# A feed-forward product in seven half-size products in place of eight

## The chip, the cores and the metric

The kernel runs on one core of a Trainium2 chip. A core has TensorE for matmuls, VectorE, ScalarE and GpSimd for elementwise work, SyncE for issuing transfers, a working memory of 128 partitions (SBUF), and eight accumulator banks (PSUM) of 128 partitions by 512 f32, into which TensorE writes. The metric is device time in microseconds; lower is better.

## The reference

A cross attention between tokens and states is followed by a two-layer feed-forward block. Cut to what matters, with B = 8 batches, H = 8 heads, S = 512 tokens, N = 32 states a head, D = 64:

```python
# x (8, 8, 512, 64), state (8, 8, 32, 64)
a = softmax(x @ state.T / 8)              # over the 32 states
xread = a @ state                         # (8, 8, 512, 64)
a2 = softmax(state @ x.T / 8)             # over the 512 tokens
sread = a2 @ x                            # (8, 8, 32, 64)
rows = concat([xread, sread], axis=2)     # 544 rows a batch, 4352 in all
X = rows.transpose(0, 2, 1, 3).reshape(4352, 512)
h = X @ w_in                              # w_in (512, 2048)
g = maximum(h, 0) + alpha * minimum(h, 0)
out = g @ w_out                           # w_out (2048, 512), out f32
```

## The kernel before

**Tiling.** The token rows of a batch are never formed as xread. Per batch the kernel computes `m` = states times `w_in` (a 256 x 2048 matrix, heads in two groups of 128 rows), and the first product is `m` transposed times the attention weights. The hidden layer lies transposed: for each of 16 blocks `jc` of 128 hidden units, a PSUM bank `h` of 128 units x 512 tokens. ScalarE writes `neg` = relu(-h), VectorE adds `neg` times (1 - alpha) to `h` and rounds to f16 (`gt`). The second product takes 128 tokens (a quarter `q`) at a time: 16 matmuls over `jc` sum into one bank of 128 x 512, which is copied to `osb` and stored. The state reads of all batches are collected in `XS` (256 rows) and pass through the same two layers as a ninth batch (`B`, number 8).

**Steps.** The order of all work is written out by hand in `ORDER`, a list of tokens such as `S.1.2.0.0` (step, batch, quarter, part, bank). Tokens are emitted one after the other; each engine runs its own instructions in that order and waits on semaphores for data and for free buffers. The PSUM bank of a tile is the last number of a token. The steps that the change and the prediction touch:

- `lx0`, `lx`, `lst`, `wi`, `wo`: loads of x, states and weights, all issued from GpSimd's queue (L161 to L203).
- `Z`: matmuls on zeros in the head, in units of 128 columns (L217).
- `xt`, `xo`: x of the first two batches transposed on TensorE (L287) and copied (L292, L295); `xd`: later batches, by a DMA transpose on SP.
- `sc` (L307), then for the tokens' softmax `sb` transpose, `smax`, `ssh`, `sexp`, `ssum`, `snorm`, `wb` (L340 to L376): VectorE, with `ssh` and `snorm` on GpSimd (L354, L368) and `sexp` on ScalarE.
- for the states' softmax `tm` (L388), `te` (L399), `tsum` (L409), `tn` (L413, a product of the weights with 1/sum on GpSimd), `tt` (DMA transpose on SP), `rd` (L432, state reads), `rdo` (L443).
- `m` (L457) and its casts `mo` (L479, on ScalarE `a` or VectorE `v`).
- `F`, `f`: first product (L490, L511; L499 for the reads); `N`: `neg` (L522); `G`: the PReLU (L530).
- `S`: two of the 16 matmuls of a quarter (L542); `O`: its copy and store (L580); `R`, `RO`: the same for the reads (L590, L600); `L`, `LO`: batch 7's last quarter in pieces of 256, 128 and 128 columns (L562, L573).

**Buffers.** Tiles take their PSUM bank by name (`k0` to `k5`, and one pair). `osb`, `neg` and `xg` have four buffers each, `m` seven.

Of the kernel before, what the change touches and what calls it, by code (L numbers as in the profile page):

```python
# [12 lines left out]
ALU = mybir.AluOpType  # L13
# [4 lines left out]
stc lx0.0 lx0.1 oma id Z.1.24 stt.0 Z.2.13 xt.0.0.0.1 sto.a xt.0.1.0.2 xo.0.0.0.v lst xo.0.1.0.v  # L18
Z.0.6 sc.0.0 xt.0.1.1.3 xt.0.0.1.4 sb.0.0 xo.0.0.1.v smax.0.0 xo.0.1.1.a str.0.5 sc.0.1 str.1.0 wi.0
sro.0.a lx.1 wi.1 ssh.p.0.0 sb.0.1 Z.1.3 sc.0 Z.5.7 m.0.0.1.2 sro.1.a sexp.0.0 smax.0.1 m.3.0.3.4  # L20
ssh.p.0.1 tm.0 mo.0.0.a.1 sexp.0.1 ssum.0.0 m.1.0.5.0 ssum.0.1 te.0.1 te.0.0 mo.1.0.v.1 wo.0
mo.1.0.a.0 snorm.p.0.0 mo.3.0.a.1 Z.2.23 xt.1.1.1.2 xt.1.0.1.2 xt.1.1.0.0 xt.1.0.0.0 mo.0.0.a.0
snorm.p.0.1 wb.0.0 mo.3.0.a.0 m.2.0 f.0.0.0.5 f.0.1.0.4 wi.2 mo.2.0.a.0 wb.0.1 mo.2.0.a.1 f.0.1.1
xo2.1.0.v N.0.1 m.0.1.1.3 f.0.0.1 mo.0.1.a.1 m.1.1 N.0.0 xo2.1.1.v mo.0.1.v.0 f.0.2.0.0 F.0.3.2
f.0.2.1 F.0.4.1 mo.1.1.v.0 mo.1.1.a.1 F.0.7.3 G.0.1 N.0.2 G.0.0 wo.1 F.0.5.4 N.0.3 G.0.2 wi.3 m.4.0
N.0.4 S.0.0.0.5 N.0.5 G.0.3 tsum.0 S.0.1.0.0 N.0.7 mo.4.0.a.1 G.0.4 S.0.0.1 S.0.1.1 G.0.5 mo.4.0.a.0
tn.0.1 m.0.2.2.1 sc.1 G.0.7 S.0.2.0.4 mo.0.2.a.0 tm.1 m.1.2.2.3 wo.2 tn.0.0 mo.0.2.a.1 mo.1.2.a.0
S.0.2.1 F.0.6.1 F.0.9.2 sb.1 lx.2 S.0.0.2 wo.3 S.0.1.2 S.0.2.2 xd.2 mo.1.2.a.1 F.0.8.3 N.0.6 N.0.9
te.1.1 G.0.6 smax.1 F.0.11.1 S.0.0.3 te.1.0 G.0.9 N.0.8 m.0.3 N.0.11 F.0.10.2 mo.0.3.a.0 S.0.1.3
# [24 lines left out]
rd.3.1 rd.2.3 O.2.0.a mo.6.0.v.1 mo.5.1.a.0 m.4.1.4.0 mo.5.1.a.1 mo.6.0.v.0 sc.5 rdo.3.a m.4.3.2.1
mo.4.1.a.1 S.2.3.6 F.3.11.0 rdo.2.a mo.4.3.a.0 wb.4 N.3.11 mo.4.1.a.0 S.2.2.0.3 F.3.0.2 mo.4.3.v.1
F.3.10.1 S.2.3.7 tm.5 S.2.2.1 S.2.2.2 G.3.11 N.3.0 F.4.1.4 sb.5 F.3.5.0 S.2.2.3 N.3.10 N.4.1 O.2.3.a
N.3.5 S.2.2.4 G.3.10 G.3.0 F.3.7.1 F.4.11.5 F.4.7.2 lx.6 G.4.1 N.4.11 N.3.7 S.2.2.5 S.2.2.6 smax.5
te.5.0 N.4.7 S.3.3.0.4 lx.7 S.2.2.7 G.3.5 ssh.p.5 S.3.3.1 O.2.2.a te.5.1 S.3.3.2 G.4.7 F.4.5.0
F.3.15.3 N.4.5 G.3.7 N.3.15 G.4.11 tn.4.0 F.4.4.2 G.4.5 S.3.1.0.1 F.3.12.5 S.3.3.3 N.4.4 G.3.15
G.4.4 N.3.12 G.3.12 sexp.5 F.4.6.0 N.4.6 S.3.3.4 ssum.5 F.4.8.3 S.3.1.1 F.4.3.2 S.3.1.2 F.4.0.5  # L60
S.3.3.5 S.3.3.6 N.4.3 S.3.3.7 N.4.8 G.4.6 N.4.0 S.3.1.3 S.3.1.4 xd.6 S.3.1.5 G.4.8 F.4.9.0 G.4.3
F.4.2.3 G.4.0 S.3.0.0.2 N.4.9 S.3.0.1 S.3.0.2 N.4.2 tsum.5 O.3.3.v S.3.1.6 G.4.9 S.3.0.3 sc.6 G.4.2
m.5.3.5.4 m.5.0.0.3 tm.6 snorm.p.5 S.3.0.4 S.3.0.5 mo.5.0.a.0 S.3.1.7 mo.5.0.a.1 mo.5.3.v.0 sb.6
mo.5.3.a.1 F.4.10.0 S.3.2.0.3 N.4.10 F.4.14.5 S.3.2.1 S.3.2.2 S.3.2.3 wb.5 N.4.14 S.3.0.6 tt.4
S.3.0.7 tn.5.1 F.5.3.4 O.3.1.a G.4.14 te.6.1 te.6.0 S.3.2.4 G.4.10 O.3.0.a m.7.2.1.5 m.5.2.0.2
# [39 lines left out]
def kernel(  # L105
# [38 lines left out]
    def single(k, name, shape, dtype):  # L144
        return ps.tile(shape, dtype, name=name, tag=f"k{k}", bufs=1)

    def two(name, shape, dtype):
        return ps.tile(shape, dtype, name=name, tag="two", bufs=1)
# [503 lines left out]
```

## Time and profile before

| | us |
|---|---|
| three runs, median (lowest to highest) | 217.57 (217.44 to 217.98) |
| span of the profiled execution | 216.3 |
| TensorE busy | 208.6 |
| VectorE busy | 164.8 |
| ScalarE busy | 137.6 |
| GpSimd busy | 71.1 |

The profile shows one execution. Of the profiled execution the span, from its first to its last instruction, is given; the time of the runs lies 1.3 us above it. "Busy" is the union of an engine's instruction intervals. A matmul's own length (379 ns for 512 columns) is longer than the spacing of matmuls in a row, as they are pipelined, so rates are read from runs of matmuls in the chain of work that ended last. PE is TensorE, PEld its weight loads, DVE is VectorE, ACT is ScalarE, POOL is GpSimd, SP is SyncE. A group line gives the busy time and mean ns of one instruction, and behind the second bar the idle time before them and what ended it.

### The profile page before, as it was taken

How to read it: one execution, taken by the hardware profiler on the slowest of the kernel's cores; microseconds unless marked ns; L12 is line 12 of the kernel's file. 1: busy time of each engine (PE TensorE's matmuls, PEld its weight loads, DVE VectorE, ACT ScalarE, POOL GpSimd, SP SyncE). 2: the span in 40 equal slices, each digit the busy share in tenths (PEclk: the TensorE clock that was granted, in tenths of full speed). 3: DMA queues.
4: the chain of work that ended last, by engine and by line, in shares of the span. 5: the costliest groups of instructions: out<-in, count | busy, mean ns of one | idle time of the engine just before them, and what ended most of it. 6: DMA issues, size and time to landing. Idle time of an engine off the chain costs nothing.

```text
span 216.3 us, 4190 instructions
## 1 busy us (share of the span) xinstructions
PE 208.6 (96%) x1637; PEld 99.3 (46%) x1637; DVE 164.8 (76%) x253; ACT 137.6 (64%) x271; POOL 71.1 (33%) x58
## 2 busy tenths in 40 slices
PE   7689999999999999999999999999999999999994
PEld 2433334444544444544444445444454455554553
DVE  3699988799999998999886869876798466665001
ACT  3399995998768957879449865566545346544021
POOL 7373858232367626314620112903500000000000
PEclk9999999999999999999999999999999999999999
DMA  6999999888475849596032532031430011110124
GB/s 82 165 202 203 205 187 184 107 240 141 47 129 167 109 88 194 100 192 149 18 83 97 134 63 100 2 97 50 52 147 27 25 48 48 48 48 4 48 100 145
DMA packets 39716, 23.12 MB, mean 107 GB/s; under 512 B 22144, under 2 KB 35984, under 8 KB 39696
## 3 DMA queue, kind: packets, MB, share of 16 engines
q0 software_dynamic: 12704, 8.62, 28.6%
q1 hardware_dynamic: 26960, 14.23, 25.4%
q8 instruction: 13, 0.21, 0.4%
q14 instruction: 7, 0.06, 0.1%
q10 hardware_dynamic: 32, 0.01, 0.0%
HBM read 17.31 MB, written 8.91 MB: 121 GB/s over the span
## 4 chain that ended last, share of the span: by engine, by line
PE 90%; DMA 5%; POOL 2%; issue 1%; ACT 0%; POOLq 0%
PE o L542 50%; PE h L490 25%; DMA w_in_sb<-in_moe_w_in_dram 5%; PE m_ps L457 4%; PE h L499 3%; PE o L590 3%; PE sr_ps L432 2%; PE o L562 2%; PE sc L307 1%; POOL xg L178 1%; POOL xg L161 0%; PE h L511 0%; POOL w_in_sb L197 0%; POOL st L191 0%; POOL ident masks.py:199 0%
## 5 line engine op out<-in xcount | busy, mean ns | idle before, releaser
L542 PE MATMUL o<-w_out_sb,gt 128*128 128x512 f16 x496 | 125.4, 379 | 0.0
L522 ACT ACTIVATE neg<-h 128x512 f32<-128x512 f32 (+1 forms) x144 | 77.6, 582 | 44.5 <-PE h L490 36.3
L530 DVE SCALAR_TENSOR_TENSOR gt<-neg,oma_sb,h 128x512 f16<-128x512 f32 x128 | 89.4, 737 | 18.7 <-ACT neg L522 18.3
L542 PEld LDWEIGHTS <-gt 128*128 128x128 f16 x496 | 47.5, 98 | 54.9 <-issue 2.9
L490 PE MATMUL h<-aT,m 128*128 128x512 f16 x250 | 68.7, 379 | 0.0
L490 PEld LDWEIGHTS <-m 128*128 128x128 f16 x250 | 24.1, 98 | 28.7 <-issue 0.9
L479 ACT CAST m<-m_ps 128x512 f16<-128x512 f32 x49 | 27.0, 603 | 6.4 <-PE m_ps L457 6.0
L413 POOL TENSOR_SCALAR e<-e,r 128x512 f16<-128x512 f16 x16 | 24.9, 1565 | 15.0 <-DVE r L409 13.8
L354 POOL TENSOR_TENSOR ts<-ts,mx 128x1024 f32<-128x1024 f32 (+1 forms) x9 | 15.5, 1719 | 42.2 <-DVE mx L348 42.2
L368 POOL TENSOR_TENSOR an<-ts,r 128x1024 f16<-128x1024 f32 (+1 forms) x9 | 15.4, 1720 | 25.2 <-DVE r L365 16.6
L580 ACT COPY osb<-o 128x512 f32<-128x512 f32 x23 | 13.7, 595 | 14.7 <-PE o L542 14.6
L457 PE MATMUL m_ps<-w_in_sb,stT 64*32 64x512 f16 x256 | 11.3, 383 | 0.5 <-DMA w_in_sb<-in_moe_w_in_dram 0.5
L399 ACT ACTIVATE e<-sc,nb 128x512 f16<-128x512 f32 x16 | 11.1, 704 | 0.4 <-DVE nb L391 0.4
L479 DVE CAST m<-m_ps 128x512 f16<-128x512 f32 x15 | 9.9, 677 | 1.4 <-PE m_ps L457 1.3
L530 DVE SCALAR_TENSOR_TENSOR gs<-neg,oma_sb,h 128x256 f16<-128x256 f32 x16 | 7.5, 476 | 4.5 <-ACT neg L522 4.5
L388 DVE TENSOR_REDUCE nb<-sc 128x2 f32<-128x1024 f32 x8 | 9.7, 1212 | 1.2 <-PE sc L307 1.2
L376 DVE STREAM_TRANSPOSE aT<-an 128x1024 f16<-128x1024 f16 (+1 forms) x9 | 10.0, 1115 | 0.7 <-POOL an L368 0.7
L364 DVE TENSOR_REDUCE r<-ts 128x32 f32<-128x1024 f32 (+1 forms) x9 | 9.8, 1089 | 0.7 <-ACT ts L360 0.7
L348 DVE TENSOR_REDUCE mx<-ts 128x32 f32<-128x1024 f32 (+1 forms) x9 | 9.8, 1090 | 0.0
L499 PE MATMUL h<-XS,w_in_sb 128*128 128x256 f16 x64 | 9.4, 273 | 0.0
L600 DVE COPY osr<-o 128x512 f32<-128x512 f32 x1 | 0.7, 692 | 11.3 <-PE o L590 11.3
L360 ACT ACTIVATE ts<-ts 128x1024 f32<-128x1024 f32 (+1 forms) x9 | 8.7, 971 | 0.0
(52 smaller groups left out, 117.6 us busy)
## 6 DMA issues: line engine op xcount, KB each, us to landing
out_dram<-osb SPq DMA_DIRECT2D x27, 256.0 KB, 2.4
xg<-in_x_dram POOLq DMA_DIRECT2D x7, 512.0 KB, 7.2
w_in_sb<-in_moe_w_in_dram POOLq DMA_DIRECT2D x4, 512.0 KB, 9.0
w_out_sb<-in_moe_w_out_dram POOLq DMA_DIRECT2D x4, 512.0 KB, 8.0
out_dram<-osb SPq DMA_DIRECT2D x9, 128.0 KB, 2.0
xg<-in_x_dram POOLq DMA_DIRECT2D x2, 256.0 KB, 4.9
out_dram<-osr SPq DMA_DIRECT2D x2, 256.0 KB, 2.5
st<-in_state_dram POOLq DMA_DIRECT2D x1, 224.0 KB, 5.6
```

What stands on the lines that cost most here:

```text
L354: engine(e).tensor_tensor(ts, ts, over_blocks(cols(live["mx", b], j, S // N)), ALU.subtract)
L368: engine(e).tensor_tensor(blocks(cols(live["an", b], j, S)), blocks(cols(live["ts", b], j, S)), over_blocks(cols(live["r1", b], j, S // N) ...
L399: nc.scalar.activation(live["e2", b][:, g, :, :], live["sc", b][:, :, :, g, :].rearrange("p r j s -> p (r j) s"), EXP, bias=live["nb", b][ ...
L413: nc.gpsimd.tensor_scalar_mul(e2, e2, live["r2", b][:, g : g + 1])
L457: nc.tensor.matmul(t[N * k : N * (k + 1), :], st_head(b, h)[64 * r : 64 * r + 64, :], w_in_sb[64 * r : 64 * r + 64, c, 512 * f : 512 * (f ...
L479: copier(e)(m_tile(b)[:, f, g, :], live["mp", b, f][g])
L490: nc.tensor.matmul(h.rearrange("p (r j s) -> p r j s", r=2, j=2), ms[b][:, f, g, 128 * j : 128 * (j + 1)], weights(b, g), start=(g == 0), ...
L499: nc.tensor.matmul(h, w_in_sb[:, c, 128 * jc : 128 * (jc + 1)], XS[:, c].rearrange("p q n b -> p (q n b)"), start=(c == 0), stop=(c == n_c ...
L522: nc.scalar.activation(neg, h, RELU, bias=0.0, scale=-1.0)
L530: nc.vector.scalar_tensor_tensor(gt, negs.pop((b, jc)), oma_sb[:, jc : jc + 1], h, ALU.mult, ALU.add)
L542: nc.tensor.matmul(outs[b, q], gts[b, jc][:, 128 * q : 128 * (q + 1)], w_out_sb[:, jc, :], start=(jc == 0), stop=(jc == n_jc - 1),)
L580: copier(e)(osb, t)
```

## The change

1. **Second product.** For batches 1 to 7 and the reads, two quarters (`qa`, `qb`), two halves of the hidden units (low, high) and two halves of the output columns are taken as a 2 x 2 by 2 x 2 block product, in seven products of 128 tokens x 1024 hidden units x 256 columns in place of eight. With A11 = (qa, low), A12 = (qa, high), A21 = (qb, low), A22 = (qb, high): s1 = A21 + A22, s2 = s1 - A11, s3 = A11 - A21, s4 = A12 - s2. These hidden sums (`A`) are f16, 128 x 512 an instruction, two for each s: 120 in all, 98 on GpSimd (`p`), 22 on VectorE (`v`). Four combinations of `w_out` are formed once (`W`, eight instructions of 1024 columns on GpSimd).
2. **Products** `P` (four matmuls of 256 columns a token). Bank x sums P1, P6, P7 and P4 in turn, and is copied out after each (`C`, 60 copies, 43 on ScalarE and 17 on VectorE); bank y holds P2, bank z P5 and then P5 + P3. VectorE adds y and z to the copies (`D`, 45). Stores are steps of their own (`st`), one of 256 KB a quarter. Batch 0 keeps `S` and `O`; the pieces of batch 7 are gone.
3. **State reads turned**: the softmax weights are the stationary side and x moves, 64 columns a matmul in four column groups in place of 32 columns in two. The result has the states on partitions, so 1/sum is applied to it (`rn`, VectorE) in place of the 16 GpSimd products `tn`; then one transpose on TensorE (`rt`) and the copy `rdo`.
4. **Heads** pair differently in the two groups (even and odd in place of 0 to 3 and 4 to 7). The second scoring of batch 0 is gone.
5. **Places**: PSUM is one tile with banks picked by number, and m, neg, gt and osb are fixed tiles with a slot number in the token. The whole order is written anew; 11 of the 15 casts of m on VectorE go to ScalarE. All output copies of batch 0 are on ScalarE.

The diff, cut:

```diff
@@ ORDER (old head, then new head; new around the last first-product blocks; new end)
-stc lx0.0 lx0.1 oma id Z.1.24 stt.0 Z.2.13 xt.0.0.0.1 sto.a xt.0.1.0.2 xo.0.0.0.v lst xo.0.1.0.v
...
+lx0.0 lst id stc oma lx0.1 wi.0 lx.1 wi.1 Z.6.8 stt.7 sto.a Z.6.20 xt.0.0.0.3 xo.0.0.0.a xt.0.1.0.4
...
+xt.1.1.0.3 xt.1.0.0.3 xo2.1.0.v m.0.1.0.1 mo.0.1.a.1.5 mo.0.1.a.0 wb.0.1 sc.1.2.4.5 tm.1 sb.1
+f.0.0.0.7 f.0.0.1 f.0.1.0.2 N.0.0.0 f.0.2.0.6 f.0.2.1 N.0.2.1 G.0.2 te.1.0 F.0.5.3 wo.1 f.0.1.1
...
+A.6.0.4.1.v.0 P.6.0.5.0.5 A.8.0.3.0.v.0 G.7.12 A.8.0.1.0.p.1 A.8.0.2.0.p.0 P.6.1.5.1 P.6.0.5.1
+C.6.1.2.a C.6.0.3.a.1 N.7.0.2 st.5.0 P.6.0.4.0 F.7.15.0 G.7.0 P.6.0.4.1 G.7.2 N.7.10.0 G.7.10
...
+D.7.0.1 D.7.1.0 P.7.0.3.0 P.7.1.3.1 A.7.0.4.1.p.1 P.7.0.3.1 D.7.0.0 P.7.1.4.0 P.7.1.4.1 D.7.0.2
+st.7.0 D.7.1.2 C.7.1.4.v st.7.2 st.7.3 P.7.0.4.1 C.7.0.4.a st.7.1
@@ state reads
-        for c in range(n_c):
-            g = c // 2
+        for g in range(2):
             for q in range(n_q):
                 r, j = divmod(q, 2)
-                for i in range(2):
-                    h = 2 * c + i
-                    k = (h - 4 * g) ^ g
+                for k in range(4):
                     nc.tensor.matmul(
-                        t[D * i : D * (i + 1), c, :],
-                        xgs[b][:, h, j, r, :],
+                        t[N * k : N * (k + 1), g, :],
                         e2T[:, g, q, N * k : N * (k + 1)],
+                        xgs[b][:, 2 * k + g, j, r, :],
...
+    def state_reads_norm(b):
+        sn = live["sn", b] = att.tile([128, 2, D], F16, name=f"sn_{b}", tag="sn", bufs=2)
+        nc.vector.tensor_tensor(sn, live.pop(("sr", b)),
+            live["r2", b].unsqueeze(2).to_broadcast([128, 2, D]), ALU.mult)
+    def state_reads_transposed(b, bk):
+        t = live["srT", b] = single16(bk, 128)
+        nc.tensor.transpose(t, live.pop(("sn", b)).rearrange("p g d -> p (g d)"), ident)
@@ second product
+    w_low, w_high = w_out_sb[:, : n_jc // 2, :], w_out_sb[:, n_jc // 2 :, :]
+    def weight_sum(i, hf, e):
...
+        a, b = {
+            0: (hi[:, :, 256:], lo[:, :, 256:]),
+            1: (lo[:, :, 256:], lo[:, :, :256]),
+            2: (hi[:, :, 256:], part.get(1)),
+            3: (hi[:, :, :256], part.get(2)),
+        }[i]
+        engine(e).tensor_tensor(part[i], a, b, ALU.subtract)
+    hc_all = consts.tile([128, 8, 2, 4, 128], F16)
+    def quarters(b, i):
+        return (2 * i, 2 * i + 1)
+    def block(b, q, f):
+        return gts[b, f][:, :, 128 * q : 128 * (q + 1)]
+    def hidden_sum(b, i, s, f, e, k):
+        qa, qb = quarters(b, i)
+        t = hc[b, i, s, f] = hc_all[:, 2 * (s - 1) + f, k]
+        x, y = {
+            1: (block(b, qb, f), block(b, qb, f + 2)),
+            2: (hc.get((b, i, 1, f)), block(b, qa, f)),
+            3: (block(b, qa, f), block(b, qb, f)),
+            4: (block(b, qa, f + 2), hc.get((b, i, 2, f))),
+        }[s]
+        engine(e).tensor_tensor(t, x, y, ALU.add if s == 1 else ALU.subtract)
+    def product(b, i, p, hf, k=None):
+        bank = {1: "x", 6: "x", 7: "x", 4: "x", 2: "y", 5: "z", 3: "z"}[p]
...
+            rows = {
+                1: lambda: hidden(b, jc, qa),
+                2: lambda: hidden(b, jc + n_jc // 2, qa),
+                3: lambda: hc[b, i, 4, hf][:, j, :],
+                4: lambda: hidden(b, jc + n_jc // 2, qb),
+                5: lambda: hc[b, i, 1, hf][:, j, :],
+                6: lambda: hc[b, i, 2, hf][:, j, :],
+                7: lambda: hc[b, i, 3, hf][:, j, :],
+            }[p]()
...
+            nc.tensor.matmul(outs[b, i, bank], rows, cols,
+                start=(p in (1, 2, 5) and jc == 0), stop=(jc == n_jc // 2 - 1), skip_group_check=True)
+    def product_out(b, i, n, e, k=None):
+        q = quarters(b, i)[n > 2]
+        half = n in (2, 3)
+        copier(e)(rows_at(b, q, k)[:, 256 * half : 256 * (half + 1)], outs[b, i, "x"])
+    def product_sum(b, i, n):
+        q, half, bank = ((0, 0, "y"), (1, 1, "z"), (0, 1, "z"))[n]
+        to = osbs[b, quarters(b, i)[q]][:, 256 * half : 256 * (half + 1)]
+        nc.vector.tensor_tensor(to, to, outs[b, i, bank], ALU.add)
+    def stored(b, q):
+        nc.sync.dma_start(token_rows(b, q), osbs[b, q])
@@ tiles
+    banks = ps.tile([128, 8, 512], F32, name="ps")
+    m_all = consts.tile([128, 14, 2, 512], F16)
+    neg_all = consts.tile([128, 4, 512], F32)
+    gt_all = consts.tile([128, 2, n_jc, S], F16)
+    osb_all = consts.tile([128, 4, d_model], F32)
```

More of the change, by code (lines that the diff above doesn't have):

```diff
@@ L141, with single, single16, two @@
     ctx.enter_context(tc.manual_schedule())
[L144 to L148, printed above, removed]
+    banks = ps.tile([128, 8, 512], F32, name="ps")
+    def single(k, w=512):
+        return banks[:, k, :w]
+    def single16(k, w):
+        return banks[:, k, :].bitcast(F16)[:, :w]
+    def two(k0, k1):
+        return banks[:, k0 : k1 + 1, :]
     def copier(e):
@@ L543, in second @@
                 outs[b, q],
[L544 removed]
+                hidden(b, jc, q),
                 w_out_sb[:, jc, :],
```

491 lines of the change are left out of this document (272 added, 219 removed).

## The prediction

> **What bounds the kernel now.** I read the page's first lines, then the groups with shapes kept apart, the stretches of ten microseconds, the chain in order of time, and the timeline of head and end. First the page: busy time, busy tenths, and the chain.
>
> ```profile
> span 216.3 us, 4190 instructions
> PE 208.6 (96%) x1637; PEld 99.3 (46%) x1637; DVE 164.8 (76%) x253; ACT 137.6 (64%) x271; POOL 71.1 (33%) x58
> ...
> PE   7689999999999999999999999999999999999994
> ...
> DVE  3699988799999998999886869876798466665001
> ...
> PEclk9999999999999999999999999999999999999999
> ...
> PE 90%; DMA 5%; POOL 2%; issue 1%; ACT 0%; POOLq 0%
> ```
>
> TensorE has no hole after the third slice, and the chain is 90% TensorE: columns streamed are time. VectorE stands at 9 through much of the first half, so it has little to give. From the stretches (busy time of each engine, instructions in brackets):
>
> ```profile
> core 0: us, PE busy (x) PEld busy (x) DVE busy (x) ACT busy (x) POOL busy (x), PEclk, DMA share, GB/s
> 0.00:10.00 10.00, 6.65 (x66) 3.14 (x68) 4.14 (x13) 2.48 (x4) 5.51 (x13) 1.00 0.85 117
> 10.00:20.00 10.00, 8.73 (x114) 3.93 (x113) 9.37 (x17) 9.72 (x20) 6.94 (x8) 1.00 1.29 202
> 20.00:30.00 10.00, 9.91 (x86) 3.76 (x84) 9.97 (x16) 9.70 (x22) 7.16 (x6) 1.00 1.24 199
> ...
> 40.00:50.00 10.00, 10.00 (x53) 4.35 (x53) 9.97 (x15) 9.97 (x23) 1.91 (x1) 1.00 0.94 179
> ```
>
> With a backlog VectorE runs at 9.97 of 10; up to 20 us it is idle 20 - 4.14 - 9.37 = 6.5 us. The three timed runs have the median 217.57 us, 1.3 above this span; I work in spans and add 1.3 at the end.
>
> **TensorE's sum.** The chain in order of time (start, length, what) gives the rates:
>
> ```profile
> 54.88 1.12 PE sr_ps L432 x64
> ...
> 74.22 1.73 PE o L542 x8
> ...
> 179.95 0.87 PE h L499 x8
> ...
> 212.42 0.91 PE o L562 x16
> ```
>
> A 512-column matmul takes 1.73/8 = 0.216 us. One of 256 columns, with a weight load of its own like the new products, takes 0.87/8 = 0.109: halving the columns loses nothing. Each pair of quarters (15: two in each of batches 1 to 7, one of the reads) goes from 32 x 0.216 = 6.92 to 56 x 0.109 = 6.09 us, so 15 x 0.83 = 12.4 us leave. Batch 7's last quarter, in pieces so far (16 of 256 columns, 32 of 128 at 0.91/16 = 0.057), gives 0.1 more: 12.5.
>
> The state reads keep 256 matmuls. Moved columns double (32 to 64) but four column groups run where two ran; row L432 is 1.12/64 = 0.0175 us each. Between no change and a doubling (+4.5) I take no change, since columns per group running at once stay 16. The eight new transposes of the reads cost 0.08 each by L287 below, 0.7 together, on the path. The second scoring of batch 0 goes (16 matmuls), but in the head, where TensorE waits for data anyway: 0. The zero matmuls stay 76 units. TensorE's line is 216.3 - 12.5 + 0.7 = 204.5.
>
> **VectorE's sum.** Groups (line, engine, operation, tile, shapes, count | busy, mean ns of one):
>
> ```profile
> L530 DVE SCALAR_TENSOR_TENSOR gt<-neg,oma_sb,h 128x512 f16<-128x512 f32 x128 | 89.4, 737 | 18.7 <-ACT neg L522 18.3
> ...
> L479 DVE CAST m<-m_ps 128x512 f16<-128x512 f32 x15 | 9.9, 677 | 1.4 <-PE m_ps L457 1.3
> ...
> L530 DVE SCALAR_TENSOR_TENSOR gs<-neg,oma_sb,h 128x256 f16<-128x256 f32 x16 | 7.5, 476 | 4.5 <-ACT neg L522 4.5
> ...
> L580 DVE COPY osb<-o 128x512 f32<-128x512 f32 x8 | 5.5, 682 | 1.8 <-PE o L542 1.8
> ...
> L295 DVE COPY xT<-xT_ps 128x1024 f16<-128x1024 f16 x2 | 1.3, 664 | 0.0
> ...
> L292 DVE COPY xT<-xT_ps 128x512 f16<-128x512 f16 x3 | 1.2, 421 | 2.7 <-PE xT_ps L287 2.7
> ...
> L600 DVE COPY osr<-o 128x512 f32<-128x512 f32 x1 | 0.7, 692 | 11.3 <-PE o L590 11.3
> ...
> L443 DVE CAST XS<-sr_ps 128x128 f16<-128x128 f32 x1 | 0.4, 444 | 0.2 <-PE sr_ps L432 0.2
> ...
> L573 DVE COPY osb<-o 128x256 f32<-128x256 f32 x1 | 0.4, 425 | 0.5 <-PE o L562 0.5
> ...
> L573 DVE COPY osb<-o 128x128 f32<-128x128 f32 x1 | 0.3, 280 | 0.0
> ```
>
> Gone from VectorE: 11 of the 15 casts of m (to ScalarE) at 9.9/15 = 0.66, 7.3; 8 output copies at 5.5/8 = 0.69, 5.5; the end's three copies 0.69 + 0.43 + 0.28 = 1.4; one XS cast 0.44; one x copy 0.42. Together 15.1.
>
> New: 45 sums of a PSUM bank into an output block, 128x256, one operand in PSUM and one in SBUF like the gs row, 7.5/16 = 0.47, 21.2; 17 copies of 128x256 at 0.43, 7.3; 8 norms of the reads at 0.28 (128 columns from PSUM), 2.2; one state copy, 0.6 by L295; 22 hidden sums. Such a sum reads two f16 operands in SBUF, which no row does: between 0.42 (the f16 copy of 512) and 0.74 (L530, two operands, 512). I take 0.42, nearest in type and size: 9.2. Together 40.5, net +25.4: VectorE's work grows from 164.8 to 190.2 us.
>
> Its line: in the new order the last hidden block, F.7.15, takes PSUM bank 0, which G.7.12 frees. Behind G.7.12 VectorE has 14 bank sums, 9 copies, 9 hidden sums and 4 PReLUs: 6.6 + 3.9 + 3.8 + 4 x 89.4/128 = 17.1. Ahead of it lie 173.1 us, plus 6.5 idle in the head: it ends at 179.6. From F.7.15 TensorE still streams 53 product steps of four matmuls, 23.1, and F.7.15 itself 0.4; from its last matmul to the span's end take 3 us (timeline of the end, below). The line is 179.6 + 23.5 + 3 = 206.1, if VectorE never idles after 20 us.
>
> **GpSimd's sum.**
>
> ```profile
> L413 POOL TENSOR_SCALAR e<-e,r 128x512 f16<-128x512 f16 x16 | 24.9, 1565 | 15.0 <-DVE r L409 13.8 <-ACT ts L360 1.1
> ...
> L354 POOL TENSOR_TENSOR ts<-ts,mx 128x1024 f32<-128x1024 f32 x7 | 13.4, 1910 | 38.2 <-DVE mx L348 38.2
> ...
> L161 POOL DMA_DIRECT2D xg<-in_x_dram x7 | 6.5, 934 | 2.3 <-PE sr_ps L432 2.3
> ...
> L354 POOL TENSOR_TENSOR ts<-ts,mx 128x512 f32<-128x512 f32 x2 | 2.1, 1050 | 4.0 <-DVE mx L348 4.0
> ```
>
> The 16 token norms leave (24.9). 98 hidden sums come, 128x512 f16: 1.05 by the same operation (L354), 1.57 by the same type (L413). I take 1.05: 102.9. Eight weight sums of 1024 elements, 1.91 each, 15.3, before batch 1's products. GpSimd goes to 164, 80% of the span. Counted from the first hidden sum TensorE has 159 us left (its steps behind that token at the rates above) and GpSimd 98 x 1.05 + 11 softmax steps x 1.91 + 3 loads x 0.93 = 127: it keeps up until a sum costs (159 - 24)/98 = 1.38 us.
>
> **ScalarE.** 11 casts, 43 half copies and one x copy come, 19 output copies, the end's copies and one state copy go:
>
> ```profile
> L479 ACT CAST m<-m_ps 128x512 f16<-128x512 f32 x49 | 27.0, 603 | 6.4 <-PE m_ps L457 6.0
> ...
> L580 ACT COPY osb<-o 128x512 f32<-128x512 f32 x23 | 13.7, 595 | 14.7 <-PE o L542 14.6
> ...
> L522 ACT ACTIVATE neg<-h 128x256 f32<-128x256 f32 x16 | 5.9, 384 | 8.0 <-PE h L499 8.0
> ...
> L287 PE MATMUL xT_ps<-ident,xg 128*128 128x128 f16 x32 | 2.5, 219 | 1.5 <-DMA xg<-in_x_dram 1.3
> ```
>
> 11 x 0.60 + 43 x 0.38 - 19 x 0.60 - about 1 = +10.6: 148 us, covered as long as nothing stands in front of a copy. That is a new wait: the four products of bank x go P1, copy, P6, copy, P7, copy, P4, copy, and the next product may not start before the copy. TensorE is in order, so a copy late behind ScalarE's N steps stops all matmuls; the order puts F, m or other products between. I cost the cover at nothing; gone, it is three waits a pair, 45 x (0.38 + some 0.2) = 26 us at most.
>
> **Head and end.** Timeline:
>
> ```profile
> 17.56 0.41 PE L457 MATMUL m_ps<-w_in_sb,stT 64*32 64x512 f16 x8 [0.51 <-DMA w_in_sb<-in_moe_w_in_dram]
> ...
> 19.32 2.71 DVE L530 SCALAR_TENSOR_TENSOR gt<-neg,oma_sb,h 128x512 f16<-128x512 f32 x4
> ...
> 23.98 1.22 DVE L388 TENSOR_REDUCE nb<-sc 128x2 f32<-128x1024 f32 x1
> ...
> 25.31 1.24 DVE L340 STREAM_TRANSPOSE ts<-sc 128x1024 f32<-128x1024 f32 x1
> ...
> 213.35 0.27 ACT L573 COPY osb<-o 128x128 f32<-128x128 f32 x1 [0.26 <-PE o L562]
> 213.65 0.33 SPq L574 DMA_DIRECT2D out_dram<-osb  x1
> ```
>
> GpSimd's first loads swap order, but the same bytes lie before the second w_in piece, so 17.56 stays. Then the new order puts batch 1's scores, maximum and transpose (1.22 + 0.1 + 1.24) on VectorE ahead of the first PReLU, which now starts near 21 rather than 19.3, while TensorE has about 2 us of first products for its banks and then waits: 1 to 3 us, I take 2. TensorE's line becomes 206.5. At the end a half copy (0.38) and 256 KB stores stand where a 0.27 copy and a small store stood: 0 to 1, in the 3 us above. The stores' issues on SP, 34 for 40, are covered.
>
> So TensorE 206.5 and VectorE 206.1 lie on one another; some of VectorE's idle time cannot be made up, and I take 207.0, with 1.3: **208.3 us**.
>
> **Rivals.** (a) TensorE alone decides and the head wait is filled: 204.5 + 1.3 = 205.8, down to 204. For it: no hole in the busy tenths now; against it: VectorE would have to be full everywhere. (b) VectorE decides clearly: a hidden sum at 0.74 (13 of them before G.7.12, +4.2), waits of 18.3 us on ScalarE as L530 has now kept in part, copies late: 212 to 217. (c) Ending slower: GpSimd's f16 sums cost what L413 shows. Then 98 x 1.57 + 24 = 178 us against TensorE's 159, +19, and 8 weight sums at up to 3.1 delay the start by up to 9.5: 204.5 + 19 + 1.3 = 225, up to 234. It decides from 1.38 us a sum (no gain is left from about 1.5). For it: same type, same engine; against it: L413 is another operation, and L354 is the operation itself. (d) VectorE's 22 sums wait for GpSimd, which is 80% busy: at most one GpSimd sum each, 13 x 1.05 = 14 us before G.7.12, half of that likely: 208.3 + 7 = 215. Now no VectorE row has two tensors in SBUF, and the GpSimd rows keep to one length (L354: 1910 ns for f32, whatever VectorE does beside it), so the rows show no such wait and cannot exclude it; my sum has none.
>
> On (d): the Trainium skill, "SBUF — State Buffer", section "Who interferes with whom", says that a VectorE instruction with two SBUF inputs contends with a GpSimd one that reads SBUF, and that the second to come is held back. By that rule the time would be near 215, by the rows 208.3; no run here shows it yet.
>
> **Chances.** Forecast, 206 to 212: 0.58. (a) below 206: 0.12. (b): 0.09 and (d): 0.07, both 212 to 217.5, of them 0.03 within 0.3% (0.65 us, about what the measurement can tell). (c): 0.14, of it 0.02 that lands faster. Range 204.5 to 217.5. Faster 0.85, same 0.03, slower 0.12.
>
> **What would show it.** Half-width products at 0.109 us each in the chain (right) or with gaps between P1, P6, P7 and P4 (copies late). The GpSimd hidden sum: about 1.05, or above 1.38. VectorE busy near 190 us and near 9.9 of 10 from 20 to 180 us. The first PReLU near 21 us with a TensorE hole of 1 to 3 us before 25. VectorE's hidden sums at 0.42 or far longer. The forecast falls if TensorE is idle for over 6 us between 25 and 200.

## The result and the profile after

The changed kernel takes 229.49 us (median of four runs, 229.29 to 229.62) beside 217.66 for the kernel before on the same chip: a ratio of 1.052 (1.049 to 1.056). The forecast was 208.3, within 204.5 to 217.5, and faster; the time lies above that range, and the kernel became slower. The first lines of the profile after:

```profile
span 227.4 us, 5041 instructions
PE 202.8 (89%) x1956; PEld 132.0 (58%) x1956; DVE 191.1 (84%) x322; ACT 143.7 (63%) x305; POOL 175.1 (77%) x148
...
PE   5976899969999979799789799988899999999992
...
DVE  2599898989799998879699899996999799875821
...
PEclk9999699999999999999999999999999999999999
...
PE 31%; DVE 16%; ACT 5%; POOL 4%; DMA 3%; issue 2%; ACTq 0%; DVEq 0%; POOLq 0%
```

TensorE has holes from the head up to the 29th slice and none behind it; its share of the chain fell from 90% to 31%. VectorE's busy time is close to the forecast (191.1 for 190.2), but it too is below 9 in many slices. The stretches from 20 to 200 us, the kernel before first, then the changed one (busy time of each engine, last of all the sum row):

```profile
20.00:45.00 25.00, 24.91 (x189) 10.35 (x187) 22.50 (x34) 21.77 (x45) 13.40 (x10) 1.00 1.13 180
...
sum 180.00, PE 179.91 PEld 84.58 DVE 149.94 ACT 123.35 POOL 58.62; mean PE 29.99 PEld 14.10 DVE 24.99 ACT 20.56 POOL 9.77
```

```profile
20.00:45.00 25.00, 22.57 (x184) 8.74 (x182) 22.70 (x33) 21.01 (x42) 21.82 (x14) 0.93 1.21 186
45.00:75.00 30.00, 27.45 (x233) 15.21 (x231) 27.93 (x42) 25.02 (x53) 26.56 (x22) 1.00 0.68 115
75.00:105.00 30.00, 27.23 (x316) 19.22 (x313) 26.62 (x42) 19.87 (x45) 27.41 (x24) 1.00 0.25 63
105.00:135.00 30.00, 25.48 (x270) 16.27 (x268) 26.67 (x40) 21.61 (x46) 23.47 (x20) 1.00 0.70 141
135.00:165.00 30.00, 27.48 (x317) 18.64 (x316) 28.02 (x48) 20.85 (x45) 24.27 (x20) 1.00 0.26 63
...
sum 180.00, PE 164.93 PEld 104.59 DVE 163.71 ACT 130.10 POOL 148.43; mean PE 27.49 PEld 17.43 DVE 27.28 ACT 21.68 POOL 24.74
```

TensorE was idle for 0.1 of these 180 us and is now idle for 15.1; 13.1 of them lie behind 25 us, where the prediction named 6 us as the sign that it falls. No engine is full: VectorE is idle for 16.3 us of the same stretch. So no single engine is the new bound; the engines wait for one another. The groups with shapes kept apart show the new work and one old step that became longer (L436, which was L391 in the kernel before; its row there comes first):

```profile
L391 DVE TENSOR_SCALAR nb<-nb 128x2 f32<-128x2 f32 x8 | 1.5, 182 | 0.3
```

```profile
L679 POOL TENSOR_TENSOR hc_all<-gt_all 128x512 f16<-128x512 f16 x48 | 56.0, 1182 | 15.1 <-DVE gt_all L573 12.3 <-PE ps L707 2.7
...
L724 DVE TENSOR_TENSOR osb_all<-osb_all,ps 128x256 f32<-128x256 f32 x45 | 17.6, 409 | 7.2 <-PE ps L707 3.7 <-ACT osb_all L719 3.5
...
L659 POOL TENSOR_TENSOR wc<-w_out_sb 128x1024 f16<-128x1024 f16 x4 | 8.5, 2134 | 0.0
...
L679 DVE TENSOR_TENSOR hc_all<-gt_all,hc_all 128x512 f16<-128x512 f16 x6 | 5.4, 918 | 0.0
L679 DVE TENSOR_TENSOR hc_all<-gt_all 128x512 f16<-128x512 f16 x8 | 5.3, 661 | 0.0
L679 DVE TENSOR_TENSOR hc_all<-hc_all,gt_all 128x512 f16<-128x512 f16 x7 | 4.5, 654 | 0.0
L436 DVE TENSOR_SCALAR nb<-nb 128x2 f32<-128x2 f32 x8 | 4.2, 519 | 0.3
```

The waits (engine, what it waited for: us in total, times, longest), those that the experiments below take up:

```profile
ACT e L444 <- DVE ts L385: 13.7, 7, 3.5
...
POOL hc_all L679 <- DVE gt_all L573: 12.3, 6, 3.6
...
ACT osb_all L719 <- DMA out_dram<-osb_all: 11.4, 5, 4.2
```

What TensorE itself waited for from 20 to 200 us, the longest entries and the one for the copies of bank x:

```profile
PE ps L537 <- DVE gt_all L573: 4.0, 4, 1.9
PE ps L537 <- ACT e L444: 2.5, 2, 1.8
PE ps L707 <- ACT e L444: 1.8, 2, 1.3
PE ps L507 <- DVE gt_all L573: 1.7, 2, 1.3
...
PE ps L507 <- ACT e L444: 0.8, 1, 0.8
...
PE ps L707 <- DVE osb_all L719: 0.4, 1, 0.4
```

For the PReLUs (L573) it is 5.9 us with a short entry of 0.2 that is not shown, for the states' exponential (L444) 5.1, and for a copy of bank x (L719) only 0.4.

One place shows how they hang together, the scores of batch 4. The timeline there, VectorE, then ScalarE, then TensorE (start, length, idle time before in brackets):

```profile
79.76 1.21 DVE L433 TENSOR_REDUCE nb<-ps 128x2 f32<-128x1024 f32 x1
81.01 0.97 DVE L436 TENSOR_SCALAR nb<-nb 128x2 f32<-128x2 f32 x1
81.89 1.24 DVE L385 STREAM_TRANSPOSE ts<-ps 128x1024 f32<-128x1024 f32 x1
...
85.89 0.75 DVE L573 SCALAR_TENSOR_TENSOR gt_all<-neg_all,oma_sb,ps 128x512 f16<-128x512 f32 x1 [1.07 <-ACT neg_all L569]
```

```profile
80.80 1.15 POOL L679 TENSOR_TENSOR hc_all<-hc_all,gt_all 128x512 f16<-128x512 f16 x1
```

```profile
83.16 0.69 ACT L444 ACTIVATE e<-ps,nb 128x512 f16<-128x512 f32 x1 [2.00 <-DVE ts L385]
...
84.50 0.37 ACT L719 COPY osb_all<-ps 128x256 f32<-128x256 f32 x1
```

```profile
84.66 0.60 PE L707 MATMUL ps<-w_out_sb,gt_all 128*128 128x256 f16 x4 [1.30 <-ACT e L444]
```

VectorE's step on 256 numbers lasts 0.97 us, until GpSimd's sum ends at 81.95. Its transpose of the scores then starts late; ScalarE, whose exponential reads the same scores, stands for 2.0 us until the transpose is done. TensorE's next product, `P.2.1.1.0.3`, writes bank 3, one of the two banks that hold these scores, and waits 1.30 us for the exponential to have read them. Behind the exponential in ScalarE's order stand the copy of a bank x (84.50) and the negatives, and VectorE itself then waits 1.07 us for the negatives.

### The profile page after: what moved, and what is told of

Read it like the earlier page. It is cut to its first block, busy times and chain, and to the rows that moved or that the text cites. A ratio compares the mean times of both kernels' runs of the same rounds, so it can differ in the third digit from the quotient of the medians.

```text
span 227.4 us, 5041 instructions
## 1 busy us (share of the span) xinstructions
PE 202.8 (89%) x1956; PEld 132.0 (58%) x1956; DVE 191.1 (84%) x322; ACT 143.7 (63%) x305; POOL 175.1 (77%) x148
## 4 chain that ended last, share of the span: by engine, by line
PE 31%; DVE 16%; ACT 5%; POOL 4%; DMA 3%; issue 2%; ACTq 0%; DVEq 0%; POOLq 0%
PE ps L707 21%; DVE gt_all L573 8%; PE ps L537 6%; DMA out_dram<-osb_all 3%; POOL hc_all L679 3%; PE ps L546 3%; ACT neg_all L569 2%; DVE hc_all L679 2%; DVE osb_all L724 1%; ACT m_all L520 1%; PE ps L507 1%; DVE ts L385 1%; DVE nb L433 1%; ACT e L444 1%; POOL ts L401 1%
## 5 line engine op out<-in xcount | busy, mean ns | idle before, releaser
L573 DVE SCALAR_TENSOR_TENSOR gt_all<-neg_all,oma_sb,ps 128x512 f16<-128x512 f32 x128 | 89.2, 736 | 6.5 <-ACT neg_all L569 6.0
L569 ACT ACTIVATE neg_all<-ps 128x512 f32<-128x512 f32 (+1 forms) x144 | 77.2, 587 | 21.7 <-PE ps L537 12.2
L537 PE MATMUL ps<-aT,m_all 128*128 128x512 f16 x250 | 68.9, 387 | 7.7 <-DVE gt_all L573 4.0
L679 POOL TENSOR_TENSOR hc_all<-gt_all 128x512 f16<-128x512 f16 x48 | 56.0, 1182 | 15.1 <-DVE gt_all L573 12.3
L707 PEld LDWEIGHTS <-hc_all 128*128 128x128 f16 x480 | 46.2, 98 | 14.0 <-issue 1.8
L707 PE MATMUL ps<-wc,hc_all 128*128 128x256 f16 x360 | 46.7, 273 | 1.1 <-DVE hc_all L679 0.7
L707 PEld LDWEIGHTS <-gt_all 128*128 128x128 f16 x336 | 32.5, 98 | 12.2 <-issue 3.3
L719 ACT COPY osb_all<-ps 128x256 f32<-128x256 f32 x43 | 16.4, 384 | 31.8 <-PE ps L707 15.7
L520 ACT CAST m_all<-ps 128x512 f16<-128x512 f32 x60 | 32.5, 609 | 3.6 <-PE ps L507 3.3
L707 PE MATMUL ps<-w_out_sb,gt_all 128*128 128x256 f16 x224 | 31.2, 273 | 1.8 <-ACT e L444 1.8
L679 POOL TENSOR_TENSOR hc_all<-gt_all,hc_all 128x512 f16<-128x512 f16 x22 | 25.7, 1183 | 2.0 <-DVE hc_all L679 1.4
L724 DVE TENSOR_TENSOR osb_all<-osb_all,ps 128x256 f32<-128x256 f32 x45 | 17.6, 409 | 7.2 <-PE ps L707 3.7
L444 ACT ACTIVATE e<-ps,nb 128x512 f16<-128x512 f32 x16 | 11.0, 692 | 13.7 <-DVE ts L385 13.7
```

The lines of the kernel that those rows point to most:

```text
L520: copier(e)(ms[b, f][:, g, :], banks[:, live["mp", b, f][g], :])
L537: nc.tensor.matmul(h.rearrange("p (r t) -> p r t", r=2), ms[b, f][:, g, 128 * j : 128 * (j + 1)], weights(b, g), start=(g == 0), stop=(g = ...
L569: nc.scalar.activation(neg, h, RELU, bias=0.0, scale=-1.0)
L573: nc.vector.scalar_tensor_tensor(gts[b, f][:, j, :], negs.pop((b, jc)), oma_sb[:, jc : jc + 1], hs.pop((b, jc)), ALU.mult, ALU.add,)
L679: engine(e).tensor_tensor(t, x, y, ALU.add if s == 1 else ALU.subtract)
L707: nc.tensor.matmul(outs[b, i, bank], rows, cols, start=(p in (1, 2, 5) and jc == 0), stop=(jc == n_jc // 2 - 1), skip_group_check=True,)
```

## The experiments

Unless said otherwise a time is a median of two runs, which lay up to 2.5 us apart, and "less" means less than the changed kernel's 229.49. The experiments ran on several chips; the kernel before, timed beside each, had medians of 217.4 to 218.2.

**All of the second product back in eight parts.** (One of its steps reads a hidden block that has been overwritten.)

```diff
-P.1.1.1.0.7 P.1.1.1.1
+S.1.3.0.7 S.1.3.1
-W.* A.* C.* D.* (all batches)
+S.* O.*
```

> All eight-product again (two quarters of 16 matmuls of 512 columns in the slots of bank x and bank z, one copy and one store a quarter), no hidden sums, no weight sums, no bank sums; all other places, the turned reads and the head as in the changed kernel. Theory V (VectorE carries too much and falls behind the order, so that PSUM banks come free late) and theory G (GpSimd's sums come late) both expect 217 to 221 us: TensorE's 12 us come back, the 17 to 22 us of gaps go, but the 5 us lost between 19 and 42 us stay. Theory P (the new order and places lose the time by themselves) expects 228 or more.

236.28 us. Without sums and bank copies it is slower by 6.8 than with the seven products. In this order the seven products are the faster ones, but the order was made for them: in one place, at 42 us, TensorE waits 4.9 us for the x transpose of batch 2. The time is where theory P has it (228 or more), but with such a wait in it the run does not show what the order costs with the seven products.

**Each kind of sum left out.** In the first two runs a product takes another hidden block in place of the sum, so what is left out is the arithmetic of those products.

```diff
-A.1.1.2.0.v.1   (22 of VectorE, or 98 with .p. of GpSimd)
+A.1.1.2.0.n.1
+        if e == "n":
+            hc[b, i, s, f] = {1: lambda: block(b, qb, f + 2), ...}[s]()
+            return
@@ third run: bank sums
-        nc.vector.tensor_tensor(to, to, outs[b, i, bank], ALU.add)
+        nc.vector.tensor_tensor(to[:, :32], to[:, :32], outs[b, i, bank][:, :32], ALU.add)
```

> The 22 hidden sums on VectorE are left out (the products take one of the two unsummed blocks, so the output is not the reference's); all else stays. VectorE has 15 us less to do. Theory V expects 8 to 12 us less: 217 to 221. Theory G expects under 3 us less: 226 or more, as GpSimd keeps its 98 sums. Theory P expects 228 or more.

> The 98 hidden sums on GpSimd are left out in the same way; the 22 on VectorE stay. Theory G expects 10 us less or more: 219 or below. Theory V expects only what VectorE gains from an undisturbed port (its sums from 0.69 to 0.42 us, its scaling of nb from 0.52 to 0.18 us, 8 to 9 us of work): 220 to 224. Theory P expects 228 or more.

> The 45 sums of a PSUM bank into an output block take 32 columns in place of 256 (the other columns miss their second term), so that every wait stays and VectorE has about 45 x 0.23 = 10 us less to do. Theory V expects 6 to 10 us less: 219 to 224. Theories G and P expect under 2 us less: 227.5 or more.

228.06, 225.38 and 227.37 us: 1.4, 4.1 and 2.1 less. Theory V's 217 to 221 fell with the first run and theory G's 219 with the second; no kind alone is the cause. Without GpSimd's sums VectorE's own change their length:

```profile
L684 DVE TENSOR_TENSOR hc_all<-gt_all 128x512 f16<-128x512 f16 x15 | 7.5, 508 | 0.0
...
L684 DVE TENSOR_TENSOR hc_all<-hc_all,gt_all 128x512 f16<-128x512 f16 x3 | 1.2, 421 | 0.0
L684 DVE TENSOR_TENSOR hc_all<-gt_all,hc_all 128x512 f16<-128x512 f16 x3 | 1.2, 418 | 0.0
```

They take 0.42 to 0.51 us in the mean instead of 0.65 to 0.92: the wait for GpSimd is real. The 4.1 us therefore hold what VectorE gains by this as well as what GpSimd's own lateness cost.

**All sums out at once.** Both edits above, for all 120 hidden sums and the 45 bank sums; here too the products read other hidden blocks in place of the sums.

> The changed kernel with all 120 hidden sums left out (the seven products read blocks that are never written) and the 45 sums of banks on 32 of 256 columns: only the new order, the seven products and the copies are left of the change, VectorE and GpSimd are as light as before. Theory P, the new order loses by itself: 219 us or more, with TensorE's holes where they were, at ScalarE's and VectorE's reads of the scores and at the PReLUs. Theory S, the sums together are what the order cannot carry although each kind alone gives only 1 to 4 us: 206 to 212 us.

221.23 us, 8.3 less. The three single gains add up to 7.6. The sums are four tenths of the 21 us between forecast and result; with the engines about as light as before, the kernel is still 1.5% slower than the one before.

**The old order in the new code.**

```diff
-(the order of the changed kernel)
+... m.3.1.1.3 rd.0.2 rn.0 rd.1.4 rn.1 sc.3.2.6.7 snorm.p.2 lx.4 rt.0.2 rdo.0.a mo.3.1.v.0.4 wb.2 rt.1.4 rdo.1.a
@@ the run after it: norm, transpose and copy of the reads later
+... m.3.1.1.3 rd.0.2 rd.1.4 rn.0 sc.3.2.6.7 snorm.p.2 lx.4 mo.3.1.v.0.4 wb.2 m.2.2.1.2 rn.1
+... F.2.5.4 N.2.1.2 F.2.3.3 rt.1.7 rt.0.6 G.2.8 S.1.3.4 snorm.p.3 F.2.11.0 rdo.1.a rdo.0.a
```

> The order of the kernel before, written with the steps of the new kernel: PSUM as one tile with numbered banks, m, neg and output blocks in fixed tiles with slot numbers, heads paired as in the new kernel, state reads turned (with their norm on VectorE and the transpose on TensorE), but the second product in eight parts and no hidden sums. Theory P1, the new order loses by itself: 217 to 219 us, as the kernel before. Theory P2, the new places (banks and slots) or the turned reads lose: 224 us or more. In the latter case TensorE shows holes in front of matmuls that write a numbered bank.

> The run before with the old order, in which the norm, transpose and copy of the turned state reads stood right behind the reads (TensorE waited there for VectorE and ScalarE: 0.8 us at 55 us, 1.9 us at 88 us), with these three steps 2 to 13 us later in the order; the second product in eight parts. Theory P1, the new order loses by itself and places and turned reads cost nothing: 217 us or less; the 64 matmuls of a batch's reads took 0.63 to 0.70 us there against 1.12 to 1.19 in the kernel before, so eight times 0.5 us less 0.5 for the transposes: 213 to 215 us. Theory P2, numbered banks and slots lose: 220 us or more.

224.58 us, and 223.71 (four runs, 221.5 to 224.8; ratio 1.026, 1.018 to 1.034). The old order does not bring 217 back, so something of the new code costs too, although the reads are shorter. Both times lie where theory P2 has them (224 or more, 220 or more), but the traces do not single out the banks. In the chain of the second run:

```profile
162.32 0.63 PE ps L442 x64
```

64 matmuls in 0.63 us, where the row of the kernel before (quoted in the prediction) has 1.12. The expectation took these 64 for one batch; they are the reads of two, as there are 256 in all, so they save 4 x 0.49 = 2.0 us and not 4. The loss lies in several small delays, for example 0.78 us at 40 us for a late x transpose and 0.85 us at 91 us for a cast on VectorE. What they have in common, numbered banks or VectorE's extra step for the reads, was not separated and stays open.

**The head.** First the maximum and the transpose of batch 1's scores behind three PReLUs, then the transpose alone, with the exponential ahead of it.

```diff
-sc.1.2.4.5 tm.1 sb.1 f.0.0.0.7 ... G.0.2 te.1.0 F.0.5.3 wo.1 f.0.1.1 N.0.1.2 smax.1 G.0.0 G.0.1 te.1.1
@@ first run
+sc.1.2.4.5 f.0.0.0.7 ... G.0.0 G.0.2 F.0.5.3 wo.1 f.0.1.1 N.0.1.2 N.0.5.3 G.0.1 tm.1 te.1.0 G.0.5 sb.1 smax.1 te.1.1
@@ second run
+sc.1.2.4.5 tm.1 f.0.0.0.7 ... G.0.2 te.1.0 te.1.1 F.0.5.3 wo.1 f.0.1.1 N.0.1.2 G.0.0 sb.1 G.0.1 smax.1
```

> The changed kernel with the maximum and the transpose of batch 1's scores on VectorE moved behind batch 0's first three PReLUs, as the kernel before had it: the head wait alone is undone. If the head's loss is a delay that carries to the end: 225 to 227 us, no idle time of TensorE between 21 and 25 us and the granted clock 1.00 from 20 to 30 us. If VectorE has to make up for it later: 229 us and the hole a few us later.

> The changed kernel with batch 1's maximum left in front, its exponential on ScalarE next, and only the transpose of the scores on VectorE moved behind two PReLUs of batch 0: the first PReLU starts 1.2 us earlier. Before, moving the maximum too left TensorE 4.3 us without work at the scores' bank and the clock fell further. If the holes at 21 to 24 us and the lower clock behind them are a loss that stays: 226 to 228 us. If the place of the hole only moves: 229 us.

The first gave 232.4 and 236.4 us, too far apart for a number. The trace, of the longer run, shows where TensorE lost; its timeline:

```profile
27.04 1.01 PE L534 MATMUL ps<-aT,m_all 128*128 128x512 f16 x2 [4.31 <-ACT e L441]
...
28.53 4.45 PE L534 MATMUL ps<-aT,m_all 128*128 128x512 f16 x10
```

A scores' bank is needed again by batch 0's hidden block 4 (`F.0.4.4`), so the later its readers come the longer TensorE waits; behind the hole, where the granted clock was 0.50, ten matmuls take 4.45 us, twice their usual time. The second gave 230.51 us, although its granted clock was 1.00 from 20 to 30 us (0.83 in the changed kernel) and TensorE's busy time there 8.22 us for 8.04: what the head gains is lost again behind it, part of it perhaps to a stretch at half clock from 114.6 to 118.0 us.

**Seven output blocks.**

```diff
-    osb_all = consts.tile([128, 4, d_model], F32)
+    osb_all = consts.tile([128, 7, d_model], F32)
-    m_all = consts.tile([128, 14, 2, 512], F16)
+    m_all = consts.tile([128, 11, 2, 512], F16)
```

> The changed kernel with seven output blocks in place of four (and eleven blocks for m in place of fourteen, to make room): ScalarE's copies no longer wait for the stores of the block's last use (11.4 us in five waits before). If these waits hold TensorE: 226 us or less. If they only fill ScalarE's idle time, as I think: 229 us.

226.95 us, 2.5 less; I had expected nothing. The waits for stores did hold TensorE. In the changed kernel, for example, a copy at 112 us waited 3.15 us for a store, negatives stood behind it, and TensorE waited 1.89 us at 114 us for a PReLU; with seven blocks both waits are gone.

**The exponential of the states away from the scores.**

```diff
-            live["sc", b][:, g],
+            live["sc", b][:, g] if b == 0 else stT[:, :512].rearrange("p (r t) -> p r t", r=2),
@@ the other run
+            live["sc", b][:, g] if b == 0 else live["ts", b][:, 512 * g : 512 * (g + 1)].rearrange(...),
```

> The changed kernel with the states' exponential of batches 1 to 7 on ScalarE reading a block of f16 in SBUF instead of the scores (the state reads are then not the reference's): ScalarE does not wait for VectorE's transpose of the same scores any more (13.7 us in seven waits), and the two banks come free after VectorE's two reads alone. If the scores' banks with three readers one after the other are what the order loses most by: 222 to 225 us. If not: 228 to 229 us, the holes then standing at PReLUs that come late.

> The changed kernel with the states' exponential of batches 1 to 7 reading VectorE's transposed copy of the scores in SBUF (the state reads are then not the reference's): ScalarE still waits for the transpose, with the casts and copies queued behind it, but does not hold the scores' two banks any more. If TensorE lost by the banks being held: 222 to 224 us, as with the exponential elsewhere. If it lost by ScalarE standing still with its queue: 228 to 230 us.

222.56 and 228.38 us. The first is 6.9 less, the largest gain of a single edit; TensorE's 5.1 us of waits for the exponential are gone. The second frees the banks after VectorE's two reads as well but keeps ScalarE's wait, and gains 1.1. Its wait:

```profile
ACT e L441 <- DVE ts L382: 12.8, 7, 3.5
```

TensorE no longer waits for the exponential there either, but its waits for PReLUs grow from 5.9 to 8.2 us: the negatives still stand behind the exponential. So freeing the banks alone does not pay. (In this run three steps of batches 2, 3 and 6 also changed places, so that the copy is read after VectorE has written it and before GpSimd changes it in place. GpSimd's idle time before that step is 8.2 us for 7.5, so this new wait explains little.)

**All three at once.**

```diff
-A.1.1.2.0.v.1
+A.1.1.2.0.n.1          (all sums; bank sums on 32 columns)
+stT[:, :512] for the exponential, seven output blocks
```

> The changed kernel with three losses taken away at once: the hidden sums left out and the bank sums narrow (alone 221.2), the states' exponential reading elsewhere (alone 222.6), seven output blocks (alone 227.0). If they are separate losses they add up: 229.5 - 8.3 - 6.9 - 2.5 = 212 us, and of the forecast's 208.3 what is left over is the head. If they are one loss seen from three sides (an engine that is late, whatever makes it so): 218 us or more.

214.42 us (ratio 0.984, 0.970 to 0.999), 15.1 less than the changed kernel; the single gains add up to 17.7. They are for the most part separate losses. Its page and its stretches:

```profile
span 211.4 us, 4908 instructions
PE 197.7 (94%) x1956; PEld 131.1 (62%) x1956; DVE 166.6 (79%) x300; ACT 143.2 (68%) x305; POOL 63.0 (30%) x50
```

```profile
20.00:45.00 25.00, 21.54 (x186) 8.58 (x184) 22.77 (x34) 21.20 (x43) 22.44 (x14) 1.00 1.22 192
45.00:75.00 30.00, 30.00 (x280) 18.07 (x281) 29.26 (x46) 26.28 (x56) 10.68 (x6) 1.00 0.85 139
75.00:105.00 30.00, 30.00 (x333) 20.03 (x310) 26.55 (x46) 25.12 (x54) 7.52 (x5) 1.00 0.50 97
105.00:135.00 30.00, 30.00 (x326) 20.93 (x325) 26.91 (x47) 26.19 (x59) 5.74 (x3) 1.00 0.36 88
```

From 45 us on TensorE is nearly full: of the 15.1 us idle between 20 and 200 us only 4.1 are left, 3.5 of them before 45. The same order thus carries the seven products; what it does not carry is the sums, the exponential's wait and the output blocks.

Some of these gains may be the clock's. The changed kernel's trace has a stretch at a granted clock of 0.50 in the head (24.95 to 28.36 us, which is 1.7 us of work); the traces without sums, with the exponential elsewhere and with all three have none before the last matmul. What such a stretch adds to the time is open: the two runs with seven output blocks had mean clocks of 0.992 and 0.997 and took 226.98 and 226.91 us.

**The exponential later, nothing left out.**

```diff
-F.1.8.3 N.1.8.0 te.2.0 te.2.1 G.1.8 ... F.1.11.7 st.0.2 st.0.0 F.1.10.0 N.1.10.2 G.1.10 F.1.2.4
+F.1.8.3 N.1.8.0 G.1.8 ... F.1.11.7 st.0.2 st.0.0 F.1.10.0 N.1.10.2 te.2.0 te.2.1 G.1.10 F.1.2.4
```

> The run with seven output blocks (227.0), and the states' exponential of batches 2 to 7 moved 1 to 3 us later in the order, behind the copies and negatives that stood behind it on ScalarE; it still comes ahead of the next writer of the scores' banks, in five batches of six now directly ahead of it (0 to 0.4 us of TensorE's work between, in place of 0.4 to 3.2). If ScalarE's standing still was the loss and the banks have room: 222 to 224 us. If the wait comes back as TensorE waiting for the banks: 226 to 228 us, with the holes in front of the banks' next writers and the exponential named there.

224.99 us, between the two: 2.0 less than with seven output blocks alone, of the 6.9 at stake. ScalarE's wait at the exponential, with seven output blocks alone and then in this run:

```profile
ACT e L441 <- DVE ts L382: 14.2, 7, 3.5
```

```profile
ACT e L441 <- DVE ts L382: 2.2, 4, 0.8
```

Most of it is gone, but TensorE's waits for the exponential grow from 5.4 to 7.0 us. The hole at 84 us, for example, was 1.30 us with seven output blocks alone and is now 1.65:

```profile
84.75 0.60 PE L704 MATMUL ps<-w_out_sb,gt_all 128*128 128x256 f16 x4 [1.65 <-ACT e L441]
```

So neither the banks freed early (1.1 us) nor ScalarE freed of most of its wait (2.0 us) comes near the 6.9, which were gained where the exponential needed neither. This is the fastest kernel found that computes all of the reference with the seven products; no such kernel beat the kernel before.

## Why the prediction was wrong, step by step

- **The products: right.** The chain at the end has

```profile
199.64 23.29 PE ps L707 x212
```

  or 0.110 us a matmul of 256 columns, for the 0.109 taken.
- **The state reads: mis-sized, to the good.** "I take no change" was the cautious middle; 64 matmuls, two batches' reads, take 0.63 us in the chain of the run above instead of 1.12, some 2 us over all 256 that the sum did not have.
- **VectorE's work: right in sum, wrong in its terms.** 191.1 for 190.2. The 45 bank sums cost 17.6 (21.2 taken), the 22 hidden sums 15.6 (9.2 taken at 0.42 each), and L436 4.2 instead of 1.5. That the sum came out is luck: the rows of VectorE's groups add up to 204.4, 30.9 more than before (173.5), where the prediction's terms add 25.4; but instructions that overlap their neighbours hide 13.3 us of the rows in the busy time, for 8.7 before.
- **GpSimd: a little short.** 1.18 us a hidden sum against 1.05, still under the 1.38 from which it would fall behind, and 2.13 a weight sum against 1.91; it is busy for 175.1 us where 164 was forecast. TensorE waited for one of its sums only once, for 0.3 us; the 4.1 us that leaving its sums out gave came by way of other waits and of VectorE's shorter steps.
- **The step that failed** is the one that put the lines together: "TensorE 206.5 and VectorE 206.1 lie on one another; some of VectorE's idle time cannot be made up, and I take 207.0". Half a microsecond stood there for all waits between engines, and VectorE's line was summed "if VectorE never idles after 20 us". It was idle for 16.3 us, TensorE for 15.1. The cover of the copies of bank x, which the prediction put "at nothing", held as such (0.4 us). The waits reached TensorE in two places that the sum does not have: at the PReLUs (5.9 us), behind ScalarE's negatives, and at the scores' banks (5.1 us), which the exponential frees only after VectorE's late transpose. The prediction saw the negatives in front of a copy, but not the exponential, or a copy that waits for a store, in front of the negatives. The runs put 6.9 us on the exponential's wait, 8.3 on the sums and 2.5 on the output blocks, 15.1 together.
- **The stores "covered": wrong**, the 2.5 us. What counted was not the issues on SP but the four output blocks, which now stay taken until two copies and one or two sums have been made.
- **Head and end: too small.** The head wait itself came as forecast: the first PReLU starts at 21.9 us (near 21 was said), and TensorE is idle for 2.0 us from 20 to 25 (2 taken). What the sum does not have is the clock behind it: ten matmuls take 4.00 us, where the rate taken gives 2.3 (10 x 0.216 and the last one's tail):

```profile
24.93 4.00 PE L537 MATMUL ps<-aT,m_all 128*128 128x512 f16 x10
```

  From the last matmul to the span's end it is 4.5 us instead of 3.0.
- **The rivals.** (a) fell. (b) named late copies, but with VectorE full as their cause and 217 as the end. (c), "ending slower", had the time (225, up to 234) but not the cause: GpSimd's sums cost 1.18 us and not 1.57. (d) was right as a mechanism and too dear in price: VectorE's sums do wait for GpSimd, yet leaving them out gave 1.4 us, not 7. The rule of the Trainium skill that was weighed there, "SBUF — State Buffer", section "Who interferes with whom", agrees with the traces: 0.65 to 0.92 us a sum with GpSimd's sums, 0.42 to 0.51 without. The same section counts `tensor_scalar` among the operations that can enter a 2-port mode, and says that an instruction in such a mode contends with GpSimd. L436 is a `tensor_scalar` and takes 519 ns against 182 before, which fits; that it ran in this mode is not shown here. No rival had the mechanism that came, slower by a ring of waits while each engine's work stayed under the span.

TensorE's line was short as well. With the reads' 2 us the rates give it some 14 us less to do, but its busy time is only 5.8 us lower, and 10.9 in the run with all three losses away. If each matmul in the trace is counted up to the start of the next, at most for its own length, the second product takes 10.6 us less (12.5 forecast) and the state reads 1.7, but the first product 3.5 more, half of it the half clock in the head, the products for `m` 2.4 more and the new transposes 0.5. A matmul's length counts in full where a hole follows; whether that is all of the rest is not settled. The run with all three losses away, at 214.4, stays 6 us above the forecast; its trace shows 3.5 us of holes from 20 to 45 us, an end of 4.4 us in place of 3.0, and first product and `m` 0.7 and 1.5 us longer than before.

## What to carry to other kernels

When three engines are each to be 60 to 90% busy, do not compare their sums only: for every instruction that waits, list what stands behind it on its own engine and who needs that, and give these waits a price, since the least loaded engine can be the one that stops the others. Ask of a product that saves multiplications by extra sums who else waits for the engines that form them, and give it more output buffers, because each output is held until its last sum. Test such a change by leaving out one suspect at a time and then all at once: here single gains of 6.9, 8.3 and 2.5 us added up to most of the 21 us that were missed, while none alone explained them.

## What the runs showed of the hardware

- **Two readers of one bank take turns.** In no trace here does ScalarE's exponential overlap VectorE's transpose of the same scores; one starts when the other has ended (83.16 behind 81.89 + 1.24 above). In the trace in which it reads another block, the two overlap ten times. The Trainium skill, "PSUM — Partial Sum Buffer", section "PSUM bank collisions raise a hardware error", says that two engines must not be in the same bank and quarter of the partitions at once, reads included, and that software has to keep them apart. The waits agree with it, 13.7 us in this kernel; no run here tried it without them.
- **A tiny VectorE step can cost a whole GpSimd sum:** 0.97 us at 81.01 for 256 numbers, ending with the GpSimd sum at 81.95. GpSimd loses little by it, 1.18 us a sum with VectorE's sums and 1.15 without.
- **Column groups at once:** four groups of 32 columns with 64 moving columns each take 0.63 us for 64 matmuls where two groups with 32 moving columns took 1.12.
- **The granted clock** fell to 0.83 from 20 to 30 us in the changed kernel, where TensorE was idle for 1.9 of the 4 us from 21 to 25 and no hole was longer than 1.18 us; it was 0.50 from 24.95 to 28.36 us. The run with eight parts had the same holes there and kept 1.00. What made the difference is not shown. The stretch in the one and in the other:

```profile
20.00:30.00 10.00, 8.04 (x42) 2.92 (x40) 9.35 (x14) 9.11 (x20) 8.32 (x7) 0.83 1.20 186
```

```profile
20.00:30.00 10.00, 8.04 (x56) 3.10 (x53) 9.47 (x14) 9.17 (x21) 4.90 (x5) 1.00 1.20 182
```
